# A fused retention and ELU-FFN kernel: four small reorderings where the work of units 3 to 9 meets the FFN

## The chip, the cores and the metric

The kernel runs on one core of a Trainium2 chip. The metric is the device time of one execution in microseconds, as the median of several runs. Engine names in the profile: PE is the matrix engine (TensorE) and PEld its weight loads, DVE is VectorE, ACT is ScalarE, POOL is GpSimd, SP is the engine that here only issues DMAs.

## The reference

There are two stages. The first is a retention layer over 8 batches, 8 heads, 576 positions and a head size of 64; the second a feed-forward layer over the 4608 resulting rows with 512 features, 2048 hidden features and an ELU.

```
scores = q @ k.T / sqrt(64)
ret    = scores * gamma_h ** (i - j)      # for i >= j, else 0
x      = (ret @ v), heads side by side    # 4608 x 512
h      = x @ w_in                         # 4608 x 2048
g      = where(h > 0, h, exp(min(h, 0)) - 1)
out    = g @ w_out                        # 4608 x 512
```

## The kernel before, in words

**Units.** The 4608 rows are cut into 36 units of 128 rows; nine units (R) cover two batches. Unit 0, 9, 18 and 27 begin a pair of batches; the fifth unit of a pair is half the end of one batch and half the start of the next, so that its loads (`place`, L48) are two halves of 64 rows. The retention of a unit is done in chunk form: masked scores inside the unit (`scores`, `masks`, `intra`), plus a product with a running state of all earlier units (`inter`), which `state` and `state_out` bring forward by one unit.

**Steps of a unit.** `load_v` and `load_qk` fetch v (issued by SP) and q, k (issued by POOL, L93). For some v buffers, VectorE first writes one element (L82), and the load waits for it. `scale_v` (POOL, L183) scales v by its decay. `turn` turns q and k: for units below 8 by transposes on TensorE and two copies out of PSUM, one half by VectorE (L205), the other by ScalarE (L206); from unit 8 by a transposing DMA that SP issues (L208). `scores` (L220) fill the PSUM tile `sc`, of which there is one; `masks` (VectorE, L232) empties it into `pt`. `inter` (L254), `intra` (L303) and `state` (L270) write the PSUM tile `o`, of which there is one too. `put_x` (VectorE, L316) scales the unit's output into the tile `xt`, the input of the FFN. `state_out` adds the new state to the running sum (VectorE, L289, L291 or L285), and a cast on ScalarE (L293, L295) makes its bf16 copy `sb`.

**FFN.** Units are grouped: units 0 to 2 form group 0; units 3, 4 and 5 are groups 1, 2 and 3 alone; units 6 and 7 are group 4, units 8 and 9 group 5; then come groups of three and, from unit 16 on, of four. `f1(g, n)` is one slot of the first matmul for group g. It fills one PSUM bank `ph` (three of them, used in turn; one further bank, `pm`, is given by name as `m`) with 512 columns, or 384 in a group of three. Behind it come e = exp on ScalarE (L387), m = e − 1 on POOL (L389), and g = min(max(h, 0), m) on VectorE (L347), which also frees the bank. The g pass is not issued at once: it is put on the list `late`, and `finish(n)` (L343) issues every g pass whose slot lies at least n slots back. `tick`, after every slot, calls `finish(3)` and then runs what `todo` holds for this slot. `ffn2(g, s)` is a quarter of the second matmul for one unit (four matmuls of 512 columns, L407); after the fourth quarter ScalarE copies the result out (L414). Units 0 to 3 use `ffn2_part` (L438) instead, which does half a unit at once, 8 matmuls, into a bank that its caller names.

**Order.** Up to f1(2, 2) the order is written out by hand: FFN1 of unit 3 (the loop over `f1(1, n)`, n = 0 to 3), then FFN2 of units 0 to 3 with the retention of units 4 and 5 between the halves. From there a planner makes a list of slots: for each group it merges the FFN1 slots of group g with the FFN2 slots of group g−1, in proportion to their number, starting with `b` FFN2 slots. The first slot of a group sets `start`, and the `due` time of each unit's `stretch` follows from it. A stretch issues the scores of unit u+1, then inter, intra, state and put_x around unit u, and puts the masks and the state sum on `todo`. Other events (loads, turns, scaling) are due at shares of the time from one unit to the next. Each engine runs its instructions in the order in which they were issued.

Of the kernel before, what the change touches and what calls it, by code (L numbers as in the profile page):

```python
# [17 lines left out]
def kernel(  # L18
# [29 lines left out]
    def place(u):  # L48

        pair, r = divmod(u, R)  # L50
        if r < 4:
            return [(0, 2 * pair, P * r, P)]
        if r == 4:
            return [(0, 2 * pair, 4 * P, 64), (64, 2 * pair + 1, 0, 64)]
        return [(0, 2 * pair + 1, 64 + P * (r - 5), P)]
# [22 lines left out]
    def load_v(u, after=None, queue=nc.sync):  # L78

        vv = raw.tile([P, H, D], FP32, name="rv", tag="rv")  # L80
        if after is not None:
            after.memset(vv[0:1, 0, 0:1], 0.0)  # L82
        for p0, b, s0, n in place(u):
            queue.dma_start(vv[p0 : p0 + n], v[b, :, s0 : s0 + n, :].rearrange("h p d -> p h d"))
        raws[u] = vv

    def load_qk(u, *cs):

        if u not in kns:
            kns[u] = qkpool.tile([P, 2, H, D], BF16, name="qkn", tag="qkn")  # L90
        for c in cs or (0, 1):
            for p0, b, s0, n in place(u):
                nc.gpsimd.dma_start(  # L93
                    kns[u][p0 : p0 + n, c], (q, k)[c][b, :, s0 : s0 + n, :].rearrange("h p d -> p h d")
                )
# [30 lines left out]
    for h in range(H):  # L126
        b, j = divmod(h, KJ)
# [40 lines left out]
    def dummy(n):  # L168

        if n:  # L170
            dum = ps_m.tile([P, 512], FP32, name="dum", tag="pm")
        for _ in range(n):
            nc.tensor.matmul(dum, warm[:, :P], warm, start=True, stop=True)  # L173
# [14 lines left out]
    def turn(u, bank=None, keys_on_v=False, between=0):  # L188

        t = tpool.tile([P, 2, HP, P], BF16, name="qkT", tag="qkT")  # L190
        n = kns[u]
        c_v = 1 if keys_on_v else 0
        if u < PE_TURNED:
            if bank:
                pool, tag = bank
                ps = [pool.tile([P, HP, P], BF16, name="tr", tag=tag) for c in range(2)]
            else:
                both = ps_s.tile([P, 2, 2, HP, P], BF16, name="tr", tag="sc")
                ps = [both[:, c, 0] for c in range(2)]
            for c in range(2):  # L200
                if c:
                    dummy(between)
                for hp in range(HP):
                    nc.tensor.transpose(ps[c][:, hp], n[:, c, 2 * hp : 2 * hp + 2].rearrange("p h d -> p (h d)"), ident)
            nc.vector.tensor_copy(t[:, c_v], ps[c_v])  # L205
            nc.scalar.copy(t[:, 1 - c_v], ps[1 - c_v])  # L206
        else:
            nc.sync.dma_start_transpose(  # L208
                t.rearrange("p c h t -> p (c h) t"), n.rearrange("p c h d -> p (c h d)")
            )  # L210
        qkTs[u] = t

    def scores(u):
        t = qkTs[u]
        sc = ps_s.tile([P, 2, HP, P], FP32, name="sc", tag="sc")
        for hp in range(HP):
            for j in range(2):
                for i in range(2):
                    r = slice(i * D, (i + 1) * D)
                    nc.tensor.matmul(  # L220
                        sc[j * 64 : (j + 1) * 64, i, hp], t[r, 1, hp, j * 64 : (j + 1) * 64], t[r, 0, hp],
                        start=(hp == 0), stop=(hp == HP - 1), skip_group_check=True,
                    )
        scs[u] = sc
# [16 lines left out]
    def inter(u):  # L241

        if u not in os_:
            os_[u] = ps_o.tile([P, 2, 512], FP32, name="o", tag="o")
        o = os_[u]
        r = u % R
        if r == 0:
            return
        n = 64 if r == 4 else P
        for a in range(2):  # L250
            for b in range(2):
                for i in range(2):
                    rows = slice(i * D, (i + 1) * D)
                    nc.tensor.matmul(  # L254
                        o[b * D : (b + 1) * D, i, a * P : a * P + n], sbs[u][rows, 2 * b + a],
                        qkTs[u][rows, 0, 2 * b + a, :n],
                        start=(a == 0), stop=False, skip_group_check=True,
                    )

    def state(u, beside):  # L260

        r = u % R
        if r == 8:
            return
        sts[u] = os_[beside][:, 1 if r == 4 else 0, 256:512].rearrange("p (c d) -> p c d", c=HP)
        rows = slice(64, P) if r == 4 else slice(0, P)
        for hp in range(HP):
            for i in range(2):
                h = 2 * hp + i
                nc.tensor.matmul(  # L270
                    sts[u][i * D : (i + 1) * D, hp], kns[u][rows, 1, h], vns[u][rows, h],
                    start=(hp == 0), stop=(hp == HP - 1), skip_group_check=True,
                )

    slot = [0]
    todo = []

    def state_out(u, cast_later=False):
        r = u % R
        if r == 8:  # L280
            return
        s = ppool.tile([P, HP, D], BF16, name="sb", tag="sb")
        sbs[u + 1] = s
        if r in (3, 7):
            nc.vector.tensor_tensor(s, sts[u], sums[u - 1], ALU.add)  # L285
            return
        sums[u] = ppool.tile([P, HP, D], FP32, name="sum", tag="sum")
        if r in (0, 4):
            nc.vector.tensor_copy(sums[u], sts[u])  # L289
        else:  # L290
            nc.vector.tensor_tensor(sums[u], sts[u], sums[u - 1], ALU.add)  # L291
        if cast_later:
            todo.append((slot[0] + 1, lambda: nc.scalar.copy(s, sums[u])))  # L293
        else:
            nc.scalar.copy(s, sums[u])  # L295

    def intra(u):
        o = os_[u]
        for a in range(2):
            for i in range(2):  # L300
                for b in range(2):
                    h = 4 * b + 2 * a + i
                    nc.tensor.matmul(  # L303
                        o[b * D : (b + 1) * D, i, a * P : (a + 1) * P], vns[u][:, h], pts[u][:, i, 2 * b + a],
                        start=(u % R == 0 and a == 0), stop=(a == 1), skip_group_check=True,
                    )
# [14 lines left out]
    def stretch(u, ahead=True):  # L321

        ahead = ahead and u + 1 < NU
        if ahead:
            scores(u + 1)
        inter(u)
        intra(u)
        if ahead:
            state(u + 1, u)
        put_x(u)  # L330
        if u + 2 < PE_TURNED:
            masks(u + 1)
        elif ahead:
            todo.append((slot[0] + 1, lambda: masks(u + 1)))
        if ahead:
            todo.append((slot[0] + 2, lambda: state_out(u + 1, True)))


    gts = {}
# [3 lines left out]
    def finish(n=0):  # L343

        while late and late[0][0] <= slot[0] - n:
            _, gt_, ph, m, _ = late.pop(0)
            nc.vector.scalar_tensor_tensor(gt_, ph, 0.0, m, ALU.max, ALU.min)  # L347
# [110 lines left out]
    h, m = (ps_h, "ph"), (ps_m, "pm")  # L458
# [33 lines left out]
    def f1(g, n, bank=None):  # L492
        k = 512 // (P * len(GROUPS[g]))
        ffn1(g, k * n, bank)
# [29 lines left out]
    for n in range(4):  # L524
        f1(1, n, m if n == 1 else None)
        if n == 0:
            state_out(3)
            load_v(4, nc.vector)
    load_qk(4)
    finish()  # L530
    load_qk(5)
    load_v(5, nc.vector)
    scale_v(4)
    nc.gpsimd.tensor_copy(gx[:, :, S:], gx[:, :, 0:64])
    for u, bank in enumerate((h, h, h, m)):
        ffn2_part(u, 0, 8, bank)
    load_qk(6)
    load_v(6, nc.vector)
# [19 lines left out]
    masks(5)  # L558
    f1(2, 0)
    f1(2, 1)  # L560
    turn(6)
    state_out(5)
    scale_v(7)
    f1(2, 2)
    load_qk(9)
    load_v(9, nc.vector)

# [2 lines left out]
    for g in range(3, NG + 1):  # L570
        f1s, f2s = [], [(ffn2, g - 1, s, 1.0) for s in range(4 * len(GROUPS[g - 1]))]
        if g < NG:
            per = 4 // len(GROUPS[g])
            f1s = [(f1, g, s, per * len(GROUPS[g]) / 4) for s in range(NFT // per)]
        else:
            f2s = f2s[:-4]
        a, b = 0, 2 if g == 4 else 0
        slots += f2s[:b]
        now += b
        start[g] = now  # L580
        while a < len(f1s) or b < len(f2s):
            if b * len(f1s) <= a * len(f2s) and b < len(f2s) or a >= len(f1s):
                slots.append(f2s[b])
                b += 1
            else:
                slots.append(f1s[a])
                a += 1
            now += slots[-1][3]
# [21 lines left out]
    for f, g, s, d in slots:  # L610
        while events and events[0][0] <= now + d / 2:
            _, kind, u = events.pop(0)
# [13 lines left out]
    u = NU - 1  # L626
# [31 lines left out]
```

## Time and profile before

| | |
|---|---|
| median of 4 runs | 313.36 us (312.09 to 313.72) |
| the profiled execution | 314.39 us |
| its span | 312.6 us |
| mean granted TensorE clock | 1.00 |
| busy: PE, POOL, DVE, ACT | 303.1, 201.8, 179.3, 123.6 us |
| DMA | 40.59 MB, mean 130 GB/s |

Times inside the profile are counted from the start of the span. In a timeline row the first number is the start, the second the length, and the brackets at the end give how long the engine was idle before and what released it; "issue" is idle time in which nothing recorded was waited for. On POOL, DVE and ACT each instruction has a row or shares one with its like (xN). The four m passes of unit 3 begin on POOL at 34.33, 35.23, 36.12 and 37.01 us; the loads of q and k of unit 4 begin at 37.57, those of unit 5 at 40.32. The first half of FFN2 of unit 0 begins on TensorE at 36.08. From unit 6 on the planner's slots fill the rest, and the last FFN2 ends a little before the end of the span.

### The profile page before, as it was taken

The numbers are of one execution on the slowest core, as the hardware profiler recorded it, in microseconds if no ns is written. First come the engines' busy times: TensorE is split into PE (matmuls) and PEld (weight loads), VectorE is DVE, ScalarE is ACT, GpSimd is POOL, SyncE is SP. The second block draws the span as 40 slices with busy tenths as digits, with TensorE's granted clock in tenths as the row PEclk, the third lists the DMA queues.
The fourth block names the chain that finished last, engine by engine and source line by source line (L and its number), as shares of the span: only waits on it lengthen the run. The fifth ranks groups of instructions, "written<-read, shape, count | busy, mean of one in ns | idle before, by whom it ended". The sixth has DMA issues, their size and how long they took to land.

```text
span 312.6 us, 7376 instructions
## 1 busy us (share of the span) xinstructions
PE 303.1 (97%) x2938; PEld 164.8 (53%) x2938; DVE 179.3 (57%) x305; ACT 123.6 (40%) x229; POOL 201.8 (65%) x292
## 2 busy tenths in 40 slices
PE   8898999999999999999999999999999999999995
PEld 3464746767766555555445444444444444444444
DVE  4557715767767666676666665666666655434300
ACT  5345403434534443344344433444344433444311
POOL 7887695988977788797777666766664433333300
PEclk9999999999999999999999999999999999999999
DMA  9999799999999999999999999999995201000112
GB/s 155 187 196 202 141 157 222 154 165 171 194 175 160 130 141 154 174 143 138 136 151 133 136 135 134 137 133 136 135 132 88 69 34 37 34 36 34 68 67 69
DMA packets 150882, 40.59 MB, mean 130 GB/s; under 512 B 141824, under 2 KB 146304, under 8 KB 150848
## 3 DMA queue, kind: packets, MB, share of 16 engines
q0 software_dynamic: 77264, 13.64, 54.9%
q1 hardware_dynamic: 72144, 24.19, 41.2%
q10 hardware_dynamic: 1440, 2.29, 2.4%
q8 instruction: 23, 0.38, 0.5%
q14 instruction: 11, 0.09, 0.1%
HBM read 36.70 MB, written 9.44 MB: 148 GB/s over the span
## 4 chain that ended last, share of the span: by engine, by line
PE 83%; DMA 6%; DVE 4%; POOL 4%; issue 1%; ACT 0%; POOLq 0%; DVEq 0%; ACTq 0%
PE ph L382 35%; PE pm L407 32%; PE pm L438 4%; PE o L303 4%; PE sc L220 3%; DMA w_in_sb<-in_moe_w_in_dram 3%; DMA qkn<-in_k_dram 3%; POOL qkn L93 2%; DVE pt L232 1%; PE o L270 1%; PE pmh L423 1%; PE o L254 1%; DVE g L347 1%; DVE xt L316 1%; POOL vn L183 1%
## 5 line engine op out<-in xcount | busy, mean ns | idle before, releaser
L389 POOL TENSOR_SCALAR m<-e 128x512 bf16<-128x512 f32 (+1 forms) x156 | 90.6, 583 | 90.3 <-ACT e L387 81.9
L382 PE MATMUL ph<-xt,w_in_sb 128*128 128x512 bf16 (+3 forms) x808 | 141.4, 313 | 3.4 <-DMA w_in_sb<-in_moe_w_in_dram 1.5
L387 ACT ACTIVATE e<-ph 128x512 f32<-128x512 f32 (+1 forms) x156 | 87.5, 564 | 140.5 <-PE ph L382 138.4
L347 DVE SCALAR_TENSOR_TENSOR g<-ph,m 128x512 bf16<-128x512 f32 (+1 forms) x156 | 99.5, 646 | 58.5 <-POOL m L389 58.1
L407 PE MATMUL pm<-w_out_sb,g 128*128 128x512 bf16 x496 | 125.6, 379 | 0.2 <-ACT ot L414 0.2
L382 PEld LDWEIGHTS <-w_in_sb 128*128 128x128 bf16 x808 | 69.3, 98 | 55.5 <-issue 3.7
L407 PEld LDWEIGHTS <-g 128*128 128x128 bf16 x496 | 47.9, 98 | 53.3 <-issue 0.6
L316 DVE TENSOR_TENSOR xt<-o,gx 128x512 bf16<-128x512 f32 x36 | 24.9, 691 | 41.9 <-PE o L270 31.9
L232 DVE TENSOR_TENSOR pt<-sc,mask 128x1024 bf16<-128x1024 f32 (+1 forms) x37 | 43.9, 1187 | 3.9 <-PE sc L220 3.9
L183 POOL TENSOR_TENSOR vn<-rv,gk 128x512 bf16<-128x512 f32 (+1 forms) x37 | 37.7, 1020 | 0.9 <-DMA rv<-in_v_dram 0.9
L93 POOL DMA_DIRECT2D qkn<-in_q_dram x39 | 35.1, 900 | 1.1 <-DMA qkn<-in_q_dram 0.4
L93 POOL DMA_DIRECT2D qkn<-in_k_dram x39 | 33.3, 856 | 0.7 <-DMA qkn<-in_k_dram 0.7
L414 ACT COPY ot<-pm 128x512 f32<-128x512 f32 x31 | 18.1, 585 | 14.1 <-PE pm L407 14.1
L220 PEld LDWEIGHTS <-qkT 64*64 64x64 bf16 x576 | 9.2, 106 | 13.7 <-issue 11.2
L220 PE MATMUL sc<-qkT 64*64 64x128 bf16 x576 | 15.0, 222 | 0.1
L303 PE MATMUL o<-pt,vn 128*64 128x128 bf16 x288 | 14.9, 225 | 0.0
L438 PE MATMUL pm<-w_out_sb,g 128*128 128x512 bf16 x64 | 14.5, 379 | 0.0
L173 PE MATMUL dum<-warm 128*128 128x512 bf16 x34 | 11.2, 464 | 1.2 <-DVE warm L119 1.2
L303 PEld LDWEIGHTS <-vn 128*64 128x64 bf16 x288 | 9.1, 109 | 3.0
L206 ACT COPY qkT<-tr 128x512 bf16<-128x512 bf16 x8 | 4.7, 583 | 14.2 <-DVE rv L82 10.7
L438 PEld LDWEIGHTS <-g 128*128 128x128 bf16 x64 | 6.0, 98 | 6.7
L270 PE MATMUL o<-vn,qkn 128*64 128x64 bf16 (+1 forms) x256 | 9.5, 196 | 0.0
(49 smaller groups left out, 98.3 us busy)
## 6 DMA issues: line engine op xcount, KB each, us to landing
rv<-in_v_dram SPq DMA_DIRECT2D x31, 256.0 KB, 5.3
out_dram<-ot SPq DMA_DIRECT2D x27, 256.0 KB, 2.4
qkn<-in_q_dram POOLq DMA_DIRECT2D x31, 128.0 KB, 4.6
qkn<-in_k_dram POOLq DMA_DIRECT2D x31, 128.0 KB, 5.5
w_in_sb<-in_moe_w_in_dram POOLq DMA_DIRECT2D x8, 256.0 KB, 9.7
w_out_sb<-in_moe_w_out_dram POOLq DMA_DIRECT2D x2, 1024.0 KB, 16.1
out_dram<-ot ACTq DMA_DIRECT2D x8, 256.0 KB, 4.4
rv<-in_v_dram SPq DMA_DIRECT2D x8, 128.0 KB, 5.3
```

The lines of the kernel that those rows point to most:

```text
L93: nc.gpsimd.dma_start(kns[u][p0 : p0 + n, c], (q, k)[c][b, :, s0 : s0 + n, :].rearrange("h p d -> p h d"))
L183: nc.gpsimd.tensor_tensor(vns[u][:, h0:h1], raws[u][:, h0:h1], gk[:, u % R, h0:h1].unsqueeze(2).to_broadcast([P, h1 - h0, D]), ALU.mult,)
L220: nc.tensor.matmul(sc[j * 64 : (j + 1) * 64, i, hp], t[r, 1, hp, j * 64 : (j + 1) * 64], t[r, 0, hp], start=(hp == 0), stop=(hp == HP - 1) ...
L232: nc.vector.tensor_tensor(pts[u][:, s].rearrange("p i h t -> p (i h) t"), scs[u][:, s].rearrange("p i h t -> p (i h) t"), m.unsqueeze(1).t ...
L303: nc.tensor.matmul(o[b * D : (b + 1) * D, i, a * P : (a + 1) * P], vns[u][:, h], pts[u][:, i, 2 * b + a], start=(u % R == 0 and a == 0), s ...
L316: nc.vector.tensor_tensor(xts[g][:, :, i * P : (i + 1) * P].rearrange("p (a i) t -> p a i t", a=2), outputs(os_[u]), gx[:, :, s0 : s0 + P] ...
L347: nc.vector.scalar_tensor_tensor(gt_, ph, 0.0, m, ALU.max, ALU.min)
L382: nc.tensor.matmul(ph[:, i * n : (i + 1) * n], w_in_sb[:, j, f : f + P], xts[g][:, j, :n], start=(j == 0), stop=(j == KJ - 1), skip_group_ ...
L387: nc.scalar.activation(e[:, w], ph[:, w], AF.Exp)
L389: nc.gpsimd.tensor_scalar(m[:, w], e[:, w], -1.0, 1.0, ALU.add, ALU.mult)
L407: nc.tensor.matmul(pm, gts[g, ft][:, it * P : (it + 1) * P], w_out_sb[:, ft], start=(ft == 0), stop=(ft == NFT - 1))
L438: nc.tensor.matmul(acc[u], gts[g, ft][:, it * P : (it + 1) * P], w_out_sb[:, ft], start=(ft == 0), stop=(ft == NFT - 1))
```

## The change

It has four parts, and the bank order goes with the first.

1. `load_qk` takes a `part`, one of the halves of a unit that is in two places. The loads of unit 4, so far issued as a block behind the four slots of f1(1, n), are issued one in each slot: q's two halves behind n = 0 and 1, k's behind n = 2 and 3. The first halves of FFN2 for units 0 to 3 take the banks h, m, h, h instead of h, h, h, m.
2. In the hand-written part, `finish(1)` stands between f1(2, 1) and `turn(6)`, so that the g passes of f1(2, 0) and f1(2, 1) are both issued on VectorE ahead of its copy of that turn; `state_out(5)` moves behind f1(2, 2).
3. In every stretch of the planner the state sum is put on `todo` for three slots later instead of two. Its cast follows one slot behind the sum as before.
4. The merge of FFN1 of group 4 (units 6 and 7) with FFN2 of group 3 (unit 5) starts with one FFN2 slot instead of two. Through `start` and `due` this also moves the stretches of units 6 and 7 forward by a slot at most: on TensorE the stretch of unit 7 now comes ahead of the first FFN2 slot of unit 5 and not behind it, an FFN2 slot lies between f1(4, 1) and f1(4, 2), and the stretch of unit 8 comes ahead of f1(4, 3) and not behind it. The rest of TensorE's order is the same.

```diff
-    def load_qk(u, *cs):
+    def load_qk(u, *cs, part=None):
...
-            for p0, b, s0, n in place(u):
+            for p0, b, s0, n in place(u) if part is None else place(u)[part : part + 1]:
                 nc.gpsimd.dma_start(
...
         if ahead:
-            todo.append((slot[0] + 2, lambda: state_out(u + 1, True)))
+            todo.append((slot[0] + 3, lambda: state_out(u + 1, True)))
...
         if n == 0:
             state_out(3)
             load_v(4, nc.vector)
-    load_qk(4)
+        load_qk(4, n // 2, part=n % 2)
     finish()
     load_qk(5)
...
-    for u, bank in enumerate((h, h, h, m)):
+    for u, bank in enumerate((h, m, h, h)):
         ffn2_part(u, 0, 8, bank)
...
     f1(2, 0)
     f1(2, 1)
+    finish(1)
     turn(6)
-    state_out(5)
     scale_v(7)
     f1(2, 2)
+    state_out(5)
     load_qk(9)
     load_v(9, nc.vector)
...
-        a, b = 0, 2 if g == 4 else 0
+        a, b = 0, 1 if g == 4 else 0
```

## The prediction

> **What bounds the kernel.** I read the page first: the span, and TensorE's share of it.
>
> ```profile
> span 312.6 us, 7376 instructions
> PE 303.1 (97%) x2938; PEld 164.8 (53%) x2938; DVE 179.3 (57%) x305; ACT 123.6 (40%) x229; POOL 201.8 (65%) x292
> ```
>
> TensorE is busy for 303.1 of 312.6 us, at a granted clock of 1.00 in every window. The table of windows puts most of the 9.5 us of idle time outside the edited stretch: about 4.6 us lie before 30 us and 2.6 us after 290 us. From 150 to 250 us it is busy for 100.00 of 100.00. So an edit between 34 and 150 us can win only what TensorE waits there. The ends of matmuls are modelled, so I take the waits from the idle time ahead of weight loads (PEld) in the timeline:
>
> ```profile
> 56.54 0.90 PEld L382 LDWEIGHTS <-w_in_sb 128*128 128x128 bf16 x16 [0.73 <-DVE rv L82]
> 60.52 0.46 PEld L204 LDWEIGHTS <-qkn 128*128 128x128 bf16 x8 [0.29 <-issue]
> 68.34 0.26 PEld L220 LDWEIGHTS <-qkT 64*64 64x64 bf16 x16 [0.42 <-issue]
> 73.24 0.75 PEld L382 LDWEIGHTS <-w_in_sb 128*128 128x128 bf16 x7 [0.60 <-issue]
> 89.62 0.53 PEld L407 LDWEIGHTS <-g 128*128 128x128 bf16 x3 [0.36 <-issue]
> 108.16 0.42 PEld L382 LDWEIGHTS <-w_in_sb 128*128 128x128 bf16 x3 [0.49 <-issue]
> 121.33 0.42 PEld L382 LDWEIGHTS <-w_in_sb 128*128 128x128 bf16 x3 [0.34 <-issue]
> ```
>
> The number in brackets is the idle time. The row at 68.34 is the ordinary switch to score matmuls while a long matmul still streams; it costs nothing and recurs at every stretch. The other six are waits, 2.81 us together. With the further 0.25 us at 136.00, all that can be won is about 3 us, 1% of the span.
>
> **Unit 4's loads, and the banks.** The four half loads (L93) leave a block behind the four m passes (37.57 to 40.3) and go one behind each m pass. POOL had 0.28 us free between these passes and an issue takes 0.70 (688 to 738 ns), so the later passes slip: m(1,1) starts at 35.6 instead of 35.23, m(1,2) at 36.9 instead of 36.12, m(1,3) at 38.15 instead of 37.01. Each g pass ends about 1.35 us after its m starts: 37.0, 38.2, 39.5. Their PSUM banks are taken by the FFN2 halves, which start on TensorE at 36.08 and then every 8 x 0.216 = 1.73 us. With the new bank order, unit 1 takes the bank of f1(1,1) at 37.8, unit 2 that of f1(1,2) at 39.5, unit 3 that of f1(1,3) at 41.3: 0.8 to 1.8 us to spare. (In the old order unit 1 would have needed 38.2 at 37.8, a wait of 0.4; the bank edit is what covers it.) On POOL all that follows is 0.7 us earlier until it runs dry at 50.9. Nobody was waiting: the turn of unit 4 starts at 44.71 with no idle time ahead of it. Value 0; bounds 0 and +0.3.
>
> A rule speaks against this edit. The Trainium skill ("SBUF — State Buffer", section "SBUF: two separate sides") says that while VectorE runs a pass that takes both its ports, GpSimd cannot write the descriptors of its DMAs, so the transfer starves. By it each issue could lie behind a g pass (0.69): three would add 2 us, g(1,3) would end at 41.6, and unit 3 would wait 0.3. The row says otherwise: the issue at 37.57, beside the g pass of 37.66 to 38.30, took 738 ns, and those from 38.3, with VectorE idle, 688 and 697. I take the row, +0.05 per issue.
>
> **ELU passes ahead of unit 6's turn copy.** The rows around it:
>
> ```profile
> 54.54 0.61 POOL L389 TENSOR_SCALAR m<-e 128x512 bf16<-128x512 f32 x1 [3.63 <-ACT e L387]
> 54.74 0.60 ACT L387 ACTIVATE e<-ph 128x512 f32<-128x512 f32 x1 [0.30 <-PE ph L382]
> 55.13 0.42 DVE L205 COPY qkT<-tr 128x512 bf16<-128x512 bf16 x1 [1.35 <-PE tr L204]
> 55.42 0.62 POOL L389 TENSOR_SCALAR m<-e 128x512 bf16<-128x512 f32 x1 [0.27 <-ACT e L387]
> 55.59 0.59 ACT L206 COPY qkT<-tr 128x512 bf16<-128x512 bf16 x1 [0.25 <-DVE qkT L205]
> 55.80 1.29 DVE L347 SCALAR_TENSOR_TENSOR g<-ph,m 128x512 bf16<-128x512 f32 x2
> 57.54 0.42 PE L220 MATMUL sc<-qkT 64*64 64x128 bf16 x16
> ```
>
> Before, VectorE does the turn copy and a sum (55.47), then both g passes; f1(2,3) needs the bank that the first g frees (0.73 us of wait, to 56.54). After, the first g starts when its m ends (55.18) and is done at 55.87, so f1(2,3) starts at 55.93: 0.6 us earlier. But the order of instructions puts *both* g passes ahead of the copy. The second needs the m of 55.42 to 56.04, so it runs 56.07 to 56.76, the copy to 57.13, and ScalarE's half of the copy, which waits for VectorE's, from 57.18 to 57.77. Scores(6) wait for that: 57.83 instead of 57.54. f1(2,3) is done at 56.8, so TensorE waits about 1.0 us there. The wait is moved and grows: **+0.29**.
>
> Here too a rule and the rows differ. The skill ("PSUM — Partial Sum Buffer", section "PSUM bank collisions raise a hardware error") says that VectorE and ScalarE clash only in one bank and quadrant and run clean in different banks; the two halves of the turn lie 2 KB apart, a bank each. By it ScalarE's copy need not wait, scores(6) would start 0.06 after 57.13, and the edit would give −0.34. But ScalarE's copy starts 0.04 us after VectorE's ends here and at 51.05 and 62.29, and the program has it wait for VectorE. I take +0.29 and keep −0.34 as the other end.
>
> Queued behind: on ScalarE, e of f1(2,2) now lies behind the delayed copy, ending at 58.35 instead of 56.98. Its m therefore starts at 58.4 instead of 57.06, and POOL, which is in order, runs 1.4 us late: unit 9's loads, the m passes, scale_v(8). Carrying this on with the rows' durations, the banks come free at 62.1 for f1(3,2) at 65.0, 64.7 for f1(3,3) at 66.8, 67.1 for f1(4,0) at 69.4, 71.1 for f1(4,2) at 72.05, 76.47 for f1(4,5) at 76.53. The least slack until 75 us is 0.9; the last has none, so I add **+0.05** (bounds 0, +0.2). SP: the memset ahead of unit 9's v load moves from 56.42 to 57.4, so the load and unit 8's transposing DMA behind it go about 0.8 later (58.2, landing 5.9 later, at 64.1; scores(8) come at 67.7). Unit 9's transposing DMA starts when its k lands, 66.1 instead of 64.75, and lands 4.2 to 6.1 later, by 72.2; scores(9) come at 73.0. No wait; with the slowest rows (7.2 for a load, 6.6 for a transpose) up to +0.8.
>
> **Unit 5's merge.** TensorE's work is the same, but one FFN2 slot (0.87) moves behind f1(4,1). Before, f1(4,0) to f1(4,2) run back to back over three banks and f1(4,3) waits for the first: from 70.02 to 73.24, or 3.22 us through e, m and g, against three slots of 0.87 and 0.02. After, an FFN2 slot and the stretch of unit 8 (0.93) lie between, and f1(4,3) comes 4.4 us after f1(4,0). **−0.60**. Stretch 7 comes a slot earlier; f1(4,0) still has one slot behind intra(7), with xt ready 0.07 before, as now.
>
> **State sums one slot later.** Two waits hang on the sum:
>
> ```profile
> 88.23 0.41 DVE L291 TENSOR_TENSOR sum<-o,sum 128x256 f32<-128x256 f32 x1
> 88.67 0.41 ACT L293 CAST sb<-sum 128x256 bf16<-128x256 f32 x1 [0.29 <-DVE sum L291]
> 88.99 0.58 ACT L414 COPY ot<-pm 128x512 f32<-128x512 f32 x1
> ```
>
> The output copy was ready at 88.6 and stands behind the cast, which waits for the sum. After, it goes ahead of the cast, ends at 89.2, and FFN2 starts on time at 89.26: **−0.36**.
>
> ```profile
> 106.09 1.22 DVE L232 TENSOR_TENSOR pt<-sc,mask 128x1024 bf16<-128x1024 f32 x1
> 107.22 0.42 DVE L291 TENSOR_TENSOR sum<-o,sum 128x256 f32<-128x256 f32 x1
> 107.55 1.01 DVE L347 SCALAR_TENSOR_TENSOR g<-ph,m 128x384 bf16<-128x384 f32 x2
> ```
>
> The first g of 107.55 frees the bank that FFN1 waits for (0.49). After, it stands ahead of the sum and ends 0.33 to 0.43 earlier; TensorE keeps about 0.06: **−0.43**. The waits at 60.52, 121.33 and 136.00 stay: the first stands behind the mask pass, the second behind mask pass and g in that order as before, the third behind an output copy whose cast, also moved, still ends just ahead of it. From 150 us TensorE waits for nothing, so no gain; the sum must leave its bank before the next stretch, some 7.9 us after the last, and comes three slots (2.6 us) behind it. Value 0, bounds 0 and +0.3.
>
> **The sum.** +0.29 + 0.05 − 0.60 − 0.36 − 0.43 = −1.05. The profiled execution took 314.39, its span 312.6 and 1.8 around it; I expect a span of 311.55. The runs' median is 313.36, 1.03 below the profiled execution, so the forecast is 313.36 − 1.05 = 312.3.
>
> **Rivals.**
> (1) The turn copy is free: ScalarE's half does not hold scores(6). −0.34 for +0.29: −1.7, 311.7. Against it stand three turns with ScalarE right behind VectorE.
> (2) The merge wins nothing, because the late POOL brings g(4,0) late too: −1.05 + 0.60 = −0.45, 312.9.
> (3) Slower: POOL's delay of 1.4 us reaches TensorE. POOL is busy for 4.7 of 5 us at 55 to 65 and 4.9 at 75 to 80, so it catches up only in the gaps between. If m of f1(3,2) to f1(4,2) lose 0.9 us more than I worked out, the slack is gone and each bank is waited for: +0.29 + 1.4 − 0.36 − 0.43 = +0.9, 314.3. For me speak 2.3 us of gaps that POOL had between 62 and 75.
>
> **Chances.** My sum 0.55, (1) 0.20, (2) 0.13, (3) 0.12. About 0.5% (1.57 us) is what a measurement of this kernel can tell from no change, and the runs shown span 1.6 us. Below 311.8 lie most of (1) and the low edge of my sum, 0.25; above 314.9 the upper part of (3), 0.07. The range goes from 311.3 ((1), with its runs' spread) to 313.9 (the DMA bound +0.8 on my sum, and the lower part of (3)).
>
> **What would show it.** TensorE's idle time at 56.5 shrinks to about 0.1 and about 1.0 appears ahead of scores(6) (57.8), released by ScalarE's turn copy; the waits at 73.24 and 89.62 are gone; at 108 less than 0.1 is left; 60.5, 121 and 136 stay. I am wrong if scores(6) start before 57.5, if a bank wait appears between 62 and 80, or if scores(9) wait for their DMA.

## The result, and the profile after

Over all runs made here the changed kernel takes 312.3 us (median of 44 runs, 311.0 to 315.77) against 313.16 us before (63 runs): a ratio of 0.9972, 95% interval 0.9961 to 0.9982. That is 0.88 us less (0.56 to 1.22). The ratio leaves out the few executions in a slower state (that of 315.77 is one). The interval lies clear of 1; the gain is 0.28%, below the 0.5% that the prediction took as its line.

The page of the changed kernel, its span and its busy times:

```profile
span 310.2 us, 7378 instructions
...
PE 301.5 (97%) x2938; PEld 164.8 (53%) x2938; DVE 179.7 (58%) x305; ACT 124.7 (40%) x229; POOL 202.2 (65%) x292
```

The span is 2.4 us shorter, nearly three times the timed gain, so the two spans must not be subtracted as they stand. The first half of FFN2 starts on TensorE at 34.62 us here and at 36.08 before. The instructions up to it are the same ones apart from the moved load issues, and in the fourteen profiles of this study that moment lies anywhere from 33.47 to 36.30 without following an edit; two executions of the changed kernel have 34.62 and 36.30. I therefore measure from it to the score matmuls of the stretch near 170 us, behind which TensorE waits for nothing: **135.15 us before (36.08 to 171.23), 134.21 after (34.62 to 168.83), −0.94**. All differences below that are called "in the trace" are of this stretch.

The idle time ahead of weight loads in the changed kernel (timeline of PEld, from 30 us to the end, without the ordinary switches of 0.42, 0.32 and 0.21):

```profile
56.31 0.26 PEld L220 LDWEIGHTS <-qkT 64*64 64x64 bf16 x16 [0.96 <-ACT qkT L206]
59.29 0.46 PEld L204 LDWEIGHTS <-qkn 128*128 128x128 bf16 x8 [0.29 <-issue]
67.88 1.62 PEld L382 LDWEIGHTS <-w_in_sb 128*128 128x128 bf16 x15 [0.15 <-issue]
105.60 0.42 PEld L382 LDWEIGHTS <-w_in_sb 128*128 128x128 bf16 x3 [0.15 <-issue]
118.78 0.42 PEld L382 LDWEIGHTS <-w_in_sb 128*128 128x128 bf16 x3 [0.34 <-issue]
133.61 0.53 PEld L407 LDWEIGHTS <-g 128*128 128x128 bf16 x3 [0.41 <-issue]
```

Add 1.46 to a time here to stand beside a time of before. The bank wait of 0.73 is gone, and scores(6) wait 0.96 for ScalarE's turn copy: +0.23. Before, scores(7) waited 0.19 for their turn copy, in a row of the timeline of PEld that the prediction did not show; that is gone.

```profile
62.93 0.26 PEld L220 LDWEIGHTS <-qkT 64*64 64x64 bf16 x16 [0.19 <-ACT qkT L206]
```

The waits of 0.60 (merge) and 0.36 (FFN2) are gone. The one at 108 went from 0.49 to 0.15. New is 0.15 ahead of f1(4, 0), at 67.88, and the wait at 136 grew from 0.25 to 0.41. The sum is +0.23 − 0.19 + 0.15 − 0.60 − 0.36 − 0.34 + 0.16 = −0.95, against −0.94 measured.

Two of these terms are too large, and the errors cancel. Weight loads run beside matmuls (from 150 to 250 us of before TensorE is busy throughout, PEld for 48.5 us), so their idle time is not quite what TensorE loses. From the start of f1(3, 1) to that of scores(7), by the matmuls, are 1.07 us before (61.86 to 62.93) and 1.00 after (60.62 to 61.62): −0.07, not −0.19. From the FFN2 slot ahead of f1(4, 0) to f1(4, 0) itself are 0.87 before and 0.91 after: +0.04, not +0.15.

The rows around the turn copy (timeline):

```profile
53.73 0.69 DVE L347 SCALAR_TENSOR_TENSOR g<-ph,m 128x512 bf16<-128x512 f32 x1 [1.40 <-POOL m L389]
...
54.61 0.69 DVE L347 SCALAR_TENSOR_TENSOR g<-ph,m 128x512 bf16<-128x512 f32 x1 [0.19 <-POOL m L389]
55.22 0.41 DVE L205 COPY qkT<-tr 128x512 bf16<-128x512 bf16 x1
...
55.67 0.59 ACT L206 COPY qkT<-tr 128x512 bf16<-128x512 bf16 x1 [1.79 <-DVE qkT L205]
...
56.31 0.42 PE L220 MATMUL sc<-qkT 64*64 64x128 bf16 x16 [0.78 <-ACT qkT L206]
...
56.84 0.62 POOL L389 TENSOR_SCALAR m<-e 128x512 bf16<-128x512 f32 x1 [1.25 <-ACT e L387]
```

Both g passes stand ahead of VectorE's copy, ScalarE sits idle for 1.79 us until that copy is done, and only then do scores(6) start. The matmuls themselves wait 0.78; about 0.2 of the 0.96 is the switch that the weight loads have anyway. POOL's next m waits 1.25 for the e that stands behind the copy.

The rows around the two state sums that mattered, near 87 us and near 105 us:

```profile
86.35 0.41 DVE L291 TENSOR_TENSOR sum<-o,sum 128x256 f32<-128x256 f32 x1
...
86.72 0.59 ACT L414 COPY ot<-pm 128x512 f32<-128x512 f32 x1 [0.21 <-PE pm L407]
...
87.39 1.03 PE L407 MATMUL pm<-w_out_sb,g 128*128 128x512 bf16 x4
...
88.27 0.40 ACT L293 CAST sb<-sum 128x256 bf16<-128x256 f32 x1
```

```profile
103.86 1.22 DVE L232 TENSOR_TENSOR pt<-sc,mask 128x1024 bf16<-128x1024 f32 x1
...
105.00 0.55 DVE L347 SCALAR_TENSOR_TENSOR g<-ph,m 128x384 bf16<-128x384 f32 x1
...
105.46 0.41 DVE L291 TENSOR_TENSOR sum<-o,sum 128x256 f32<-128x256 f32 x1
...
105.60 0.42 PEld L382 LDWEIGHTS <-w_in_sb 128*128 128x128 bf16 x3 [0.15 <-issue]
```

In the first, the output copy now goes ahead of the cast, and FFN2 follows it without a pause. In the second, the g pass stands ahead of the sum; it ends at 105.55 and the weight load follows at 105.60. What is left of this wait (0.15) lies behind the mask pass, not behind the sum.

### The profile page after: what moved, and what is told of

It reads as the page before. It is cut to its first block, busy times and chain, and to the rows that moved or that the text cites. A ratio compares the mean times of both kernels' runs of the same rounds, so it can differ in the third digit from the quotient of the medians.

```text
span 310.2 us, 7378 instructions
## 1 busy us (share of the span) xinstructions
PE 301.5 (97%) x2938; PEld 164.8 (53%) x2938; DVE 179.7 (58%) x305; ACT 124.7 (40%) x229; POOL 202.2 (65%) x292
## 4 chain that ended last, share of the span: by engine, by line
PE 87%; DMA 8%; DVE 1%; POOL 1%; ACT 1%; issue 1%; SPq 0%; POOLq 0%; DVEq 0%; ACTq 0%
PE ph L382 37%; PE pm L407 34%; DMA w_in_sb<-in_moe_w_in_dram 6%; PE pm L438 4%; PE o L303 4%; PE sc L220 4%; DMA rv<-in_v_dram 2%; PE o L270 1%; PE pmh L423 1%; PE o L254 1%; PE tr L204 1%; POOL m L389 0%; DVE g L347 0%; DVE pt L232 0%; SPq L114 0%
## 5 line engine op out<-in xcount | busy, mean ns | idle before, releaser
L414 ACT COPY ot<-pm 128x512 f32<-128x512 f32 x31 | 18.2, 586 | 14.1 <-PE pm L407 14.1
L220 PEld LDWEIGHTS <-qkT 64*64 64x64 bf16 x576 | 9.2, 106 | 14.1 <-issue 10.8
L438 PE MATMUL pm<-w_out_sb,g 128*128 128x512 bf16 x64 | 14.5, 379 | 0.0
L173 PE MATMUL dum<-warm 128*128 128x512 bf16 x34 | 10.3, 430 | 1.2 <-DVE warm L119 1.2
```

What stands on the lines that cost most here:

```text
L220: nc.tensor.matmul(sc[j * 64 : (j + 1) * 64, i, hp], t[r, 1, hp, j * 64 : (j + 1) * 64], t[r, 0, hp], start=(hp == 0), stop=(hp == HP - 1) ...
L438: nc.tensor.matmul(acc[u], gts[g, ft][:, it * P : (it + 1) * P], w_out_sb[:, ft], start=(ft == 0), stop=(ft == NFT - 1))
```

## The experiments

Each edit is made to the changed kernel. The ratio is to the kernel before, in runs on the same chip, with its 95% interval. The trace column is the stretch defined above; before has 135.15, and the changed kernel 134.21.

| edit | median us | ratio | stretch in the trace |
|---|---|---|---|
| e1: turn edit undone | 311.91 | 0.9976 (0.9954 to 0.9999) | 133.93 |
| e2: one g pass ahead of the turn copy, not two | 311.15 | 0.9947 (0.9922 to 0.9973) | 134.11 |
| e3: merge edit undone | 312.96 | 0.9997 (0.9968 to 1.0026) | 134.78 |
| e4: state sums as before | 312.69 | 0.9990 (0.9965 to 1.0016) | 135.03 |
| e5: bank order of before | 312.25 | 0.9977 (0.9960 to 0.9993) | 134.74 |
| e6: loads and banks of before | 312.09 | 0.9981 (0.9961 to 1.0001) | 134.37 |
| e7: ScalarE's turn copy issued first | 311.41 | 0.9958 (0.9938 to 0.9977) | 133.66 |
| e8: e2 and unit 9's loads earlier | 310.82 | 0.9947 (0.9928 to 0.9965) | 133.32 |
| a0: the changed kernel again | 312.16 | 0.9965 (0.9946 to 0.9984) | 135.12 |
| e2b: e2 again | 311.56 | 0.9957 (0.9938 to 0.9976) | 133.36 |
| e8b: e8 again | 311.54 | 0.9945 (0.9924 to 0.9966) | 133.48 |
| e9: e8 and a later cast | 311.03 | 0.9947 (0.9922 to 0.9971) | 134.45 |

The intervals are ±0.5 to ±0.9 us wide, so the parts, each worth 0.1 to 0.9 us, are told apart by the waits in the traces, and the times only bear witness to the larger ones.

**The turn edit undone (e1).**

```diff
-    finish(1)
     turn(6)
+    state_out(5)
     scale_v(7)
     f1(2, 2)
-    state_out(5)
```

> The kernel after, with the turn of unit 6 put back ahead of both ELU passes. My account (each wait is local and the edits add up): the wait ahead of scores(6), 0.96 us after, is gone and the 0.73 us ahead of f1(2,3) is back, so it is 0.2 to 0.3 us FASTER than the kernel after: about 1.1 us under before. Rival (the turn edit is what helps, because the g pass of f1(2,0) comes early): 0.6 us slower than after. Rival (the edits only work together): no change against after, the 0.2 us being given back at the next turn.

The row of its timeline (PEld) that answers to 56.54 before:

```profile
55.08 0.90 PEld L382 LDWEIGHTS <-w_in_sb 128*128 128x128 bf16 x16 [0.73 <-DVE rv L82]
```

The old bank wait is back with its old 0.73, the wait of scores(6) is gone, and so is the 0.15 ahead of f1(4, 0): 0.28 less in the trace than with the edit, of which 0.23 stands at scores(6) and 0.04 at f1(4, 0). The turn edit by itself is a loss in these traces; the timed difference to the changed kernel is too small for its interval.

**Half of the turn edit (e2, e2b).** Only the g pass that frees the bank goes ahead of the copy:

```diff
-    finish(1)
+    finish(2)
     turn(6)
```

> The kernel after, with finish(2) for finish(1) ahead of the turn of unit 6: only the g pass of f1(2,0) goes ahead of the copy. My account: f1(2,3) still starts at once, the copy no longer waits for the second m, and the wait of 0.96 us ahead of scores(6) shrinks to about 0.1; 0.85 us faster than after, 1.7 under before (about 311.4 us). Rival (the copies are not what holds scores(6), or POOL's delay behind it catches up with TensorE): 0 to 0.3 us faster than after.

> One pass ahead of the turn copy, once more: does the 0.99 us wait of scores(9) for the transposing DMA come back? If it is the landing time of that DMA (4.2 to 7.0 us seen), the wait is anything from 0 to 1 us and the stretch from the first FFN2 half to the scores near 170 takes 133.1 (no wait) to 134.1 (as before). If it is the order of the program, the wait is 0.9 to 1.1 again. Timed: 1.3 to 1.9 us below before.

Neither the bank wait nor the wait of scores(6) is left, in both traces. But the first one has a wait that was in no trace so far, and the second has it much smaller. The row of each (timelines of PEld, e2 first, then e2b):

```profile
70.91 0.26 PEld L220 LDWEIGHTS <-qkT 64*64 64x64 bf16 x16 [0.99 <-DMA qkT<-qkn]
```

```profile
71.91 0.26 PEld L220 LDWEIGHTS <-qkT 64*64 64x64 bf16 x16 [0.23 <-DMA qkT<-qkn]
```

Scores(9) wait for unit 9's transposing DMA. 0.21 of it is the switch that they have anyway, so it costs 0.8 in one and nothing in the other. Without it both traces give 133.3, 0.9 less than the changed kernel. The times say the same direction twice: −1.66 us (−2.4 to −0.8) and −1.35 us (−1.9 to −0.8) against before, where the changed kernel has −0.88; the intervals overlap its own.

**The merge edit undone (e3).**

```diff
-        a, b = 0, 1 if g == 4 else 0
+        a, b = 0, 2 if g == 4 else 0
```

> The kernel after, with the merge of unit 5 starting with two FFN2 slots again. My account: the wait of about 0.6 us ahead of f1(4,3) is back and no other changes: 0.6 us slower than after, 0.3 under before. Rival (the merge wins nothing of its own, since m, g and bank come late with the delayed POOL anyway): within 0.2 us of after; or, if POOL's delay of 1.4 us adds to it, a wait of 1 us or more there and slower than before.

The timeline of PEld in this kernel, at f1(4, 3):

```profile
73.27 0.75 PEld L382 LDWEIGHTS <-w_in_sb 128*128 128x128 bf16 x7 [0.61 <-issue]
```

The bank wait returns with 0.61. The whole stretch is 0.57 longer. Timed, the gain of the change is all but gone, though the interval (0.9968 to 1.0026) still holds the 0.9972 of the change.

**The state sums two slots late again (e4).**

```diff
-            todo.append((slot[0] + 3, lambda: state_out(u + 1, True)))
+            todo.append((slot[0] + 2, lambda: state_out(u + 1, True)))
```

> The kernel after, with the state sum back at two slots. My account: the waits of 0.36 us (FFN2 near 87 us) and 0.49 us instead of 0.15 (FFN1 near 105 us) are back, that of 0.41 us near 133 falls to 0.25: 0.5 us slower than after, 0.35 under before. Rival (the later sum helps all through the kernel, by freeing VectorE for g passes): 1 us or more slower than after, with waits at many stretches. Rival (it does nothing): as after.

The rows of its timeline (PEld) that the changed kernel does not have, or has smaller:

```profile
61.44 0.26 PEld L220 LDWEIGHTS <-qkT 64*64 64x64 bf16 x16 [0.45 <-ACT qkT L206]
87.54 0.53 PEld L407 LDWEIGHTS <-g 128*128 128x128 bf16 x3 [0.36 <-issue]
106.07 0.42 PEld L382 LDWEIGHTS <-w_in_sb 128*128 128x128 bf16 x3 [0.49 <-issue]
```

The waits of 0.36 and 0.49 are back. The first row is one that the prediction lacks: with the turn edit in and the sum two slots late, the sum stands on VectorE ahead of the copy of turn 7, and scores(7) wait 0.45 (their matmuls start 0.33 later than in the changed kernel). The later sum removes that too. In the trace this part of the change is worth 0.82, where 0.5 was expected.

**The banks, and the loads (e5, e6).** e5 keeps the spread loads and takes the old bank order; e6 puts back both.

```diff
-    for u, bank in enumerate((h, m, h, h)):
+    for u, bank in enumerate((h, h, h, m)):
```

```diff
-        load_qk(4, n // 2, part=n % 2)
+    load_qk(4)
```

> The kernel after, with the banks h, h, h, m as before but unit 4's loads still split over the slots. My account: unit 1's first half of FFN2 must wait for the g pass of f1(1,2), which POOL's loads have pushed back to about 0.5 us behind that half's start; a wait of 0.4 to 0.6 us appears 1.7 us into FFN2 of unit 0 and all that follows on TensorE is as much later: 0.5 us slower than after. Rival (the delay is taken back at scores(6), where TensorE waits for VectorE, ScalarE and POOL anyway): as after.

> The kernel after, with unit 4's loads as one block behind the slots again, and the old banks with them. My account: nobody waits for these loads, so every wait of TensorE from 34 us on is as in the kernel after, to 0.1 us; as after. Rival (the loads start up to 2.6 us earlier, and the transfers of units 4 to 9 with them, which is worth something later): slower than after by 0.3 us or more, with a DMA wait at a turn or at scores(8) or (9).

The new row of e5's timeline (PEld), then that of e6's:

```profile
37.94 6.57 PEld L438 LDWEIGHTS <-g 128*128 128x128 bf16 x31 [0.67 <-issue]
```

```profile
43.99 0.24 PEld L204 LDWEIGHTS <-qkn 128*128 128x128 bf16 x4 [0.17 <-issue]
```

With the loads spread and the old banks, the second FFN2 half waits for its bank: +0.53 on the stretch. The bank edit does cover the load edit. With both put back that wait is not there; the second half of the turn of unit 4 waits 0.17 for its loads, and the stretch is 0.16 longer. The trace of before has the same loads without this wait. The last load of k landed up to 5.5 us after its issue in e6 and up to 5.2 before: here the old place of the loads has no time to spare. Timed, neither can be told from the changed kernel.

**Who holds ScalarE's copy (e7).** For unit 6 alone the two copies of the turn change their order of issue:

```diff
+            if u == 6:
+                nc.scalar.copy(t[:, 1 - c_v], ps[1 - c_v])
...
-            nc.scalar.copy(t[:, 1 - c_v], ps[1 - c_v])
+            if u != 6:
+                nc.scalar.copy(t[:, 1 - c_v], ps[1 - c_v])
```

> The kernel after, with ScalarE's half of the turn copy of unit 6 issued ahead of VectorE's, so that it waits for TensorE alone and VectorE's waits for it. If it is only the order in which the two copies are issued that makes ScalarE wait, its copy runs beside the two ELU passes, e of f1(2,2) comes 1.4 us earlier, and the wait ahead of scores(6) falls from 0.96 to about 0.35 (the end of VectorE's copy, then 0.06): 0.6 us faster than after. Rival (the two copies cannot run apart, or scores(6) are held by the ELU passes alone): 0.96 stays.

The timeline of this kernel around the turn copy:

```profile
52.58 0.69 DVE L350 SCALAR_TENSOR_TENSOR g<-ph,m 128x512 bf16<-128x512 f32 x1 [1.40 <-POOL m L392]
52.63 0.58 ACT L206 COPY qkT<-tr 128x512 bf16<-128x512 bf16 x1
...
53.47 0.69 DVE L350 SCALAR_TENSOR_TENSOR g<-ph,m 128x512 bf16<-128x512 f32 x1 [0.20 <-POOL m L392]
...
54.07 0.41 DVE L207 COPY qkT<-tr 128x512 bf16<-128x512 bf16 x1
...
54.54 0.42 PE L223 MATMUL sc<-qkT 64*64 64x128 bf16 x16 [0.16 <-DVE qkT L207]
```

(Line numbers behind 205 are up to 3 higher here.) ScalarE's copy runs beside VectorE's g pass, takes its usual 0.58, and is done 0.86 us before VectorE's copy starts. Scores(6) now wait 0.16 and not 0.78, and the stretch is 0.55 shorter. So ScalarE's half needs nothing of VectorE's; it waited because the program issues it second.

**Unit 9's loads earlier (e8, e8b).** e2, and `load_qk(9)` moved ahead of f1(2, 2):

```diff
     scale_v(7)
+    load_qk(9)
     f1(2, 2)
     state_out(5)
-    load_qk(9)
     load_v(9, nc.vector)
```

> As e2_one_pass_ahead, and load_qk(9) ahead of f1(2,2). In the profile of e2 TensorE waited 0.99 us at scores(9) for unit 9's transposing DMA, which took back what was won at scores(6). Here the loads of unit 9 fill the gap of 1.2 us that POOL has ahead of m of f1(2,2), and start about 1.4 us earlier. My account: the wait at scores(9) is gone or under 0.2 us, and from the first FFN2 half on TensorE is 1.8 us ahead of the kernel before: about 311.3 us. Rival (the transposes are late because the DMA engines are full, not because the loads are issued late): 0.5 us or more of the wait stays. Rival (m and g of f1(2,2) and f1(2,3), now 0.9 us later, hold a bank): a new wait near 62 us.

> One pass ahead, and unit 9's loads ahead of f1(2, 2), once more: again no wait at scores(6) or scores(9), and 133.3 us from the first FFN2 half to the scores near 170. Against the kernel without the earlier load in the same call: 0 us if the DMA wait is rare, up to 1 us less if it is the rule.

The first trace has no wait at scores(6) or scores(9), and 133.32. The second has 0.36 at scores(9), 0.15 of it beyond the switch, which "again no wait" did not foresee. Timed beside e2b on the same chip, it shows no difference: 0.9945 and 0.9957, each ±0.002.

**The changed kernel again (a0).** No edit.

> The changed kernel once more, for a second trace. My account: from the first FFN2 half on TensorE to the score matmuls of the stretch near 170 us it takes 134.2 us again, to 0.1, with the same waits (0.96 ahead of scores(6), 0.15 near 105, 0.34 near 119, 0.41 near 133); only the time up to the first FFN2 half moves, between 33 and 36 us. The rival, that executions also differ inside this stretch, shows 0.3 us or more beside 134.2. Timed: 0.9 us below before.

My account of a constant stretch failed here: 135.12, not 134.2. The waits at 56, 67, 105, 118 and 133 us came back to the hundredth (0.96, 0.15, 0.15, 0.34, 0.41). One was added, 0.90 beyond the ordinary switch, and it is the whole difference (timeline of PEld):

```profile
74.04 0.26 PEld L220 LDWEIGHTS <-qkT 64*64 64x64 bf16 x16 [1.11 <-DMA qkT<-qkn]
```

It is scores(9) again. Unit 9's k load and its transposing DMA, by the timelines of POOL and SP, first in the first execution of the changed kernel and then in this one:

```profile
58.35 0.88 POOL L93 DMA_DIRECT2D qkn<-in_k_dram  x1
...
64.03 1.24 SPq L208 DMA_TRANSPOSE qkT<-qkn  x1
```

```profile
60.04 0.88 POOL L93 DMA_DIRECT2D qkn<-in_k_dram  x1
...
66.98 2.03 SPq L208 DMA_TRANSPOSE qkT<-qkn  x1
```

From the issue of the load to that of the transpose (SP waits for the landing) are 5.7 us in one and 6.9 in the other; the transpose then landed 7.1 us later here (74.04 less 66.98). Load and transpose together took 14.0 us. In the first execution the transpose landed 4.8 us after its issue, load and transpose together took 10.5, and TensorE, which reached scores(9) 13.1 us after the issue of the load, did not wait.

**The cast behind the output copy (e9).** e8, and the cast of the state sum three slots behind the sum:

```diff
-            todo.append((slot[0] + 1, lambda: nc.scalar.copy(s, sums[u])))
+            todo.append((slot[0] + 3, lambda: nc.scalar.copy(s, sums[u])))
```

> As the kernel with unit 9's loads ahead, and the cast of the state sum three slots behind the sum and not one, so that ScalarE's output copy near 133 us goes ahead of the cast. My account: the wait of 0.41 there falls to 0.1 to 0.25, all else stays; 0.2 to 0.3 us less from the first FFN2 half to the scores near 170. The rival: the cast, now elsewhere, stands ahead of another exp or output copy, or inter waits for it, and a new wait gives it back: 0 to +0.4.

The timeline of this place before the change, then in the changed kernel, then in e9, with its wait at scores(9) ahead:

```profile
134.30 0.40 ACT L293 CAST sb<-sum 128x256 bf16<-128x256 f32 x1
...
135.36 0.59 ACT L414 COPY ot<-pm 128x512 f32<-128x512 f32 x1 [0.28 <-PE pm L407]
```

```profile
132.67 0.40 ACT L293 CAST sb<-sum 128x256 bf16<-128x256 f32 x1
...
132.97 0.59 ACT L414 COPY ot<-pm 128x512 f32<-128x512 f32 x1
```

```profile
73.00 0.26 PEld L220 LDWEIGHTS <-qkT 64*64 64x64 bf16 x16 [1.49 <-DMA qkT<-qkn]
...
134.35 0.59 ACT L414 COPY ot<-pm 128x512 f32<-128x512 f32 x1
...
134.99 0.53 PEld L407 LDWEIGHTS <-g 128*128 128x128 bf16 x3 [0.25 <-issue]
...
135.45 0.40 ACT L293 CAST sb<-sum 128x256 bf16<-128x256 f32 x1
```

The wait falls from 0.41 to 0.25, which is the upper end of what was expected. What stays is the wait of before: there the copy had waited for TensorE alone, and it starts 1.06 us after the start of its FFN2 slot both there and in e9 (134.30 to 135.36, 133.29 to 134.35), against 1.22 in the changed kernel (131.75 to 132.97). But this execution has 1.28 at scores(9) beyond the switch, and so 134.45. Without that it would be 133.2. Timed, it is the same as e8.

**The best version.** The five runs with one pass ahead of the copy (e2, e2b, e8, e8b, e9) have 0.9945 to 0.9957 of the time before, 1.3 to 1.7 us less; the changed kernel has 0.9972. Each of their intervals still overlaps that of the changed kernel, so that they are faster than it rests on all five lying below it and on the waits in the traces. They cannot be told from one another, nor from e7 (0.9958), so the edit of e2, one number in one line, is what the runs support.

## Why the prediction was right, step by step

The forecast (312.3) was met, and its sum of −1.05 stands beside −0.94 in the first trace and −0.88 (−1.22 to −0.56) timed. Single terms were off and partly made up for each other. That the median agrees to the digit is luck: over all runs the kernel before takes 313.16, 0.20 less than the 313.36 that the forecast started from, and the gain was 0.17 smaller than the sum. In the second trace of the changed kernel a DMA wait takes back nearly all of the gain (135.12 against 135.15).

- **Turn edit, +0.29: right in mechanism and nearly in size.** The bank wait went, both g passes came ahead of the copy, scores(6) waited for ScalarE's copy: +0.23. With the 0.04 at f1(4, 0) that it also causes, e1 makes it a loss of 0.28.
- **The rule on PSUM banks** (the Trainium skill, "PSUM — Partial Sum Buffer", section "PSUM bank collisions raise a hardware error"). I took the rows, which had ScalarE waiting for VectorE, and for the change as it stands that was the right sum. e7 shows why the rule is not refuted by them: ScalarE copied out of its bank of the turn while VectorE's g pass read another bank, in its usual 0.58, so the wait comes from the order of issue. (No run here has the two halves of one turn copied at the same time.) Rival (1) (turn copy free) thus fails for this change, and is to be had by swapping two lines.
- **Bank of f1(4, 5), +0.05: wrong place.** No bank wait came there. POOL's delay reached TensorE through `put_x(7)` instead: its g pass ahead of it on VectorE waited for a late m (0.71 us), and f1(4, 0), which the prediction called ready 0.07 before, waited: 0.15 by its weight loads, 0.04 by its matmuls.
- **Merge, −0.60: right** (e3: 0.61 of wait, 0.57 of stretch). Rival (2), that it wins nothing, falls.
- **State sums, −0.36 and −0.43.** The first is exact. The second is −0.34: I left 0.06 and 0.15 is left, behind the mask pass. Two things near it were missed. The sum leaving its place ahead of the copy of turn 7 takes away the wait of 0.19 there, which with the other parts in and the sum two slots late would be 0.45 (e4). And "136 stays" was wrong: I saw that the cast would end just ahead of the output copy, and did not see that it now sits directly in front of it, which made 0.25 into 0.41. e9 moves the cast and gets 0.16 back.
- **Loads and banks, 0: right**, within 0.16. The old order would have cost 0.4 by my working and costs 0.53 (e5).
- **The rule on issues beside VectorE** (the Trainium skill, "SBUF — State Buffer", section "SBUF: two separate sides"). The row was right again, and the rule was set against this edit without need: the section names passes of VectorE in a two-port performance mode or with two SBUF inputs, these only against a GpSimd operation that reads SBUF. The g pass reads h from PSUM and only m from SBUF, and no run here shows it in such a mode, so these issues do not test the rule. Two of the four in the changed kernel, each beside a g pass (timeline):

```profile
33.44 0.74 POOL L93 DMA_DIRECT2D qkn<-in_q_dram  x1
33.53 0.69 DVE L347 SCALAR_TENSOR_TENSOR g<-ph,m 128x512 bf16<-128x512 f32 x1 [0.40 <-POOL m L389]
...
34.78 0.69 POOL L93 DMA_DIRECT2D qkn<-in_q_dram  x1
34.87 0.69 DVE L347 SCALAR_TENSOR_TENSOR g<-ph,m 128x512 bf16<-128x512 f32 x1 [0.65 <-POOL m L389]
```

  They take 0.69 to 0.74, against 0.69 to 0.70 with VectorE idle before; none lies behind a pass of 0.69.
- **Rival (3), POOL's delay reaching TensorE bank by bank, did not come.** The delay was real (m of f1(2, 2) starts 1.24 us later, counted from the first FFN2 half), but through the banks and `put_x(7)` it cost 0.04 between 62 and 80. It reached TensorE by another way, unit 9's loads.
- **Scores(9), "no wait, up to +0.8": half right, and the weakest step.** I listed such a wait as a sign of being wrong. The first execution has none, the second has 0.90, and both are the same program. The cause is margin: from the issue of k to the time when TensorE is ready for scores(9) are 15.6 us before (58.57 to 74.20) and 13.1 after. Two parts of the change share in this, which a sum of separate terms does not show. The turn edit puts the issue 1.24 us later, counted from the first FFN2 half, and the merge, which moves the stretch with scores(9) ahead of f1(4, 3), brings scores(9) 1.29 earlier. With the turn edit undone (e1) the margin is 14.1, with the merge undone (e3) 14.5.

  Against this stands how long load and transpose of unit 9 take, from the issue of k to the landing of the transpose (the profile gives the landing of each DMA; where TensorE waits, its weight load follows within 0.1). Over all fourteen traces, whether TensorE waited or not, this is 9.8 to 15.3 us: 10.4 before, 10.5 and 13.9 in the two executions of the changed kernel, 13.9 and 13.1 in e2 and e2b, 12.5 and 14.2 in e8 and e8b, 15.3 in e9. In seven of the fourteen it is more than 13.1, in none more than 15.6. e8 gives a margin of 14.1, which was enough in one of the three executions with it (e9 included). The prediction took its durations from one profile and kept the spread as a bound, when it should have been a cost with a chance. The bound was too small as well: its slowest transpose was 6.6, where the whole trace of before has one of 8.3.

What stays open is how often this wait comes. If every run lost 0.9 there, the change would gain nothing; if none did, 0.94. The timed −0.88 (−1.22 to −0.56) allows a mean loss of up to 0.38 us, and only two traces of the changed kernel exist. What makes one landing slow and another fast was not tested.

## What to carry to other kernels

Where a pass is moved ahead of another on an engine in order, move only the one that somebody waits for: one g pass freed the bank, and the second only delayed the copy, the e behind it, and a DMA behind that. Where two engines share a copy, look at which half is issued first before you believe that one needs the other. Count the margin of every DMA that a change brings closer to its user, in us from issue to need, for all parts of the change together, and set it beside the spread of landing times over several profiles and not beside one.

## What was not expected of the hardware

- The time to the first FFN2 half moved between 33.47 and 36.30 us from execution to execution; behind it the stretch of 134 us repeated to some hundredths, but for the one DMA wait. A difference of two spans of 2.4 us meant 0.94.
- Load and transpose of one unit took 9.8 to 15.3 us over fourteen profiles, and 10.5 and 13.9 in two executions of one program. A wait for them shows up in one profile of a program and not in the next, and it is the only part of the stretch, as TensorE sees it, that was seen to change between executions of one program.
